# A windowed attention and a two-layer MLP on one core: other loads, exponentials and output order for the first batch

## The chip, the core and the metric

The kernel runs on one core of a Trainium2 chip. That core has TensorE (PE in the profile; PEld is its loading of weights), VectorE (DVE), ScalarE (ACT), GpSimd (POOL) and SyncE (SP). Here POOL issues nearly all transfers from HBM, because they change float32 to float16 on the way; SP issues the copies within SBUF of the first two batches and the output's stores. Sixteen DMA engines move the bytes of all queues. The metric is device time in microseconds (us), from launch to the last store.

## The reference

Eight batches, eight heads, 576 tokens, 64 numbers a head. Every query sees 32 keys: in heads 0 to 3 the 32 latest tokens, in heads 4 to 7 every fourth token back to 128. The rows of all heads then go through a two-layer MLP.

```python
rel = pos[:, None] - pos[None, :]
mask_plain = (rel >= 0) & (rel < window)
mask_dil = (rel >= 0) & (rel < window * dilation) & (rel % dilation == 0)
scores = np.where(masks[None], scale * q @ k.transpose(0, 1, 3, 2), -1e9)
attn = np.exp(scores - scores.max(-1, keepdims=True))
attn = attn / (attn.sum(-1, keepdims=True) + 1e-9)
x = (attn @ v).transpose(0, 2, 1, 3).reshape(B * S, H * D)   # 4608 x 512
h = x @ w_in                                                 # 512 x 2048
out = (h / (1 + np.exp(-h))) @ w_out                         # 2048 x 512
```

## The kernel before, in words

The order of instructions is written out by hand: each engine executes in the order of the Python calls. The plain heads are called z = 0, the dilated ones z = 1; for z = 1 the tokens are sorted into four classes, so that a class's window is contiguous. For each batch and z there are these steps: PE turns q and k (transposes against an identity), DVE and ACT copy them to `qT`, `kT` (z = 0) or `qC`, `kC` (z = 1); PE makes the scores; DVE scales, masks and finds the maximum (`ms`, `nm`); ACT takes the exponentials (`exps`, L459); DVE divides (`normal`, L472 to L475); PE turns the result (`turn`, L484), DVE copies it (`turned`, L492); PE multiplies with v (`values`); DVE copies into `xT` (`finish`).

`exps` has two forms. Where `shift` has subtracted the maximum on DVE (L441), one ACTIVATE covers all keys (L453) and the sums are a DVE reduction (L468). Otherwise ACT does one ACTIVATE with an accumulator for each block of 64 keys (L459), 8 to 12 for a part.

The MLP of a batch is `layer1` (16 groups of 128 hidden units, PE into a `big` PSUM tile, Silu on ACT into `gT`) and `layer2` (tiles of 128 tokens, 16 matmuls of 512 columns each, DVE copy, store by SP). `big` has 2 buffers of two banks, `ps` 4 of one bank. While the MLP of one batch runs, `plan_of(b)` puts the attention steps of later batches between its matmuls: `at(s, fn, ...)` runs `fn` at step s, where steps 0 to 15 are layer 1's groups and each step from 16 on is four matmuls of layer 2.

Batch 0 has nothing to hide behind, and is cut in two parts: tokens 0 to 255 and 256 to 575. Its layer 1 runs by part (`layer1_part`, L625; part 0 has steps -16 to -1, part 1 steps 0 to 15), and starts when the values of part 0 are in `xT`. Ahead of it stand, in this order on POOL's queue: q and k of part 0 (heads 4 to 7, then 0 to 3, `load_qk0`, L119), those of part 1, v of batch 0 (`load_v`: two dilated blocks L127, two short ones L134, the plain heads L138), four quarters of w_in (L175), q and k of batch 1 (L102), four quarters of w_out (L181), v of batch 1. A transfer of part 0 fills 32 partitions, one of part 1 fills 40. v arrives in the upper partitions of `vw`; `shift_v` copies it to the lower ones (L148, L153, L156, L158), for batch 0 on SP's queue in two groups, FIRST (what part 0 needs) and REST. `keep_busy` (L796) issues matmuls of the identity whose result nobody reads.

Of the kernel before, what the change touches and what calls it, by code (L numbers as in the profile page):

```python
# [8 lines left out]
F16 = mybir.dt.float16  # L9
F32 = mybir.dt.float32  # L10
# [4 lines left out]
P = 128  # L15
W = 32
DIL = 4
# [5 lines left out]
UR = 8  # L23
# [4 lines left out]
def kernel(  # L28
# [62 lines left out]
    def load_qk(b):  # L91

        for which in (0, 1):
            t = nat.tile([P, H * UR, D], F16, tag=f"n{which}", name=f"n{which}_{b}")
            u0, u1 = 2 * URS[0], 2 * (URS[0] + URS[1])
            qk[b, 0, which] = t[:, 0:u0].rearrange("p (h u) d -> p h u d", h=2)
            qk[b, 1, which] = t[:, u0:u1].rearrange("p (h u) d -> p h u d", h=2)
        for z in (1, 0):
            for which, src in ((1, k), (0, q)):
                for i in (0, 1):  # L100
                    h = 2 * (2 * z + i)
                    nc.gpsimd.dma_start(  # L102
                        out=qk[b, z, which][i * HF : i * HF + UPS[z]].rearrange("p h u d -> p h (u d)"),
                        in_=src[b, h : h + 2].rearrange("h (p u) d -> p h (u d)", u=URS[z]),
                    )

    def load_qk0(part, halves):

        t0, n = ((0, PA), (SA, PB))[part]
        if part not in qk0:  # L110
            qk0[part] = [
                nat.tile([P, H * UR, D], F16, tag=f"n{i}", name=f"n{i}_0{part}").rearrange(
                    "p (h u) d -> p h u d", h=H
                )
                for i in (0, 1)
            ]
        for h0, h1 in halves:
            for dst, src in ((qk0[part][1], k), (qk0[part][0], q)):
                nc.gpsimd.dma_start(  # L119
                    out=dst[0:n, h0:h1],  # L120
                    in_=src[0, h0:h1, t0 : t0 + n * UR].rearrange("h (p u) d -> p h (u d)", u=UR),
                )

    def load_v(b):
        vw = vws[b % 2]
        for m in (0, 1):
            nc.gpsimd.dma_start(  # L127
                out=vw[KB:P, NP + m * ND : NP + (m + 1) * ND].rearrange("p (h r) d -> p h (r d)", r=DIL),
                in_=v[b, HH:H, m * DIL * KB : (m + 1) * DIL * KB].rearrange("h (p r) d -> p h (r d)", r=DIL),
            )  # L130
        lo = CL - W - TL
        for n in (0, 1):
            c = NP + 2 * ND + 2 * n * DIL
            nc.gpsimd.dma_start(  # L134
                out=vw[n * KB : n * KB + W + TL, c : c + 2 * DIL].rearrange("p (h r) d -> p h (r d)", r=DIL),
                in_=v[b, HH + 2 * n : HH + 2 * n + 2, lo * DIL : S].rearrange("h (p r) d -> p h (r d)", r=DIL),
            )
        nc.gpsimd.dma_start(  # L138
            out=vw[KB:P, 0:NP].rearrange("r (h m) d -> r h m d", h=HH),
            in_=v[b, 0:HH].rearrange("h (m r) d -> r h m d", r=KB),  # L140
        )

    def shift_v(b, queue, parts):

# [49 lines left out]
    band = cpool.tile([P, KB], F32, name="band")  # L194
    nc.vector.memset(band[0:W], 0.0)
    clear_v(0, nc.vector)
    load_qk0(0, ((HH, H),))
    make_identity(nc, ident)

    nc.gpsimd.affine_select(  # L200
# [4 lines left out]
        out=band[0:W], in_=band[0:W], compare_op=ALU.is_ge, fill=NEG,  # L205
        base=W, pattern=[[-1, KB]], channel_multiplier=1,
    )
    load_qk0(0, ((0, HH),))
    load_qk0(1, ((HH, H), (0, HH)))
    load_v(0)  # L210
    shift_v(0, nc.sync, (FIRST, REST))
    for c in range(4):
        load_w_in(c)

    for kt, kc, qc in zip(kTs, kCs, qCs):
# [269 lines left out]
                t[:, i, :], a["pn", z, hi][:, 2 * i : 2 * i + 2].rearrange("p t c -> p (t c)"), ident  # L485
            )

    def turned(b, z, hi):
        a = att(b)
        n = width(b, z, hi) // 2  # L490
        pt = a["pt", z, hi] = ptp.tile([P, WM // 2, P], F16, tag="pt", name=f"ptT_{b}_{z}_{hi}")
        nc.vector.tensor_copy(pt[:, 0:n], a["ptT", z, hi][:, 0:n])  # L492

    def values(b, z):

# [52 lines left out]
            a["xs", z] = [ps.tile([P, 2, QB], F32, tag="ps", name=f"xs_0_{z}_0")]  # L548
            last_values(0, z, (0,))

    def finish0(z, part, copy=nc.vector.tensor_copy):
        a = att(0)
        run = QB * (DIL if z else 1)
        for e in (0, 1):
            f = lambda y: y.rearrange("d n (m e c) -> d n m e c", e=2, c=run)[:, :, :, e, :]
            copy(f(a["xT"][:, 2 * z : 2 * z + 2, part * SA : part * SA + SA]), f(a["x", z][e]))
        if part:
            last_finish(0, z, 0, copy)

    def last_values(b, z, es):  # L560

# [56 lines left out]
    def layer1_part(f, part):  # L618
# [12 lines left out]
                )  # L631
        nc.scalar.activation(gT[:, f : f + 2, c0:c1], h[:, :, 0 : c1 - c0], AF.Silu)  # L632

    def layer2(b, plan):

        tiles = range(0, 4) if b % 2 == 0 else range(4, 9)
        for x, t in enumerate(tiles):
            o = big.tile([P, 2, 512], F32, tag="big", name=f"o_{b}_{t}")[:, 0]
            for f in range(NFF):
                if f % 4 == 0:  # L640
                    plan(NFF + 4 * x + f // 4)
                nc.tensor.matmul(  # L642
                    o,
                    gT[:, f, t * P : (t + 1) * P],
                    w_out16[:, f, :],
                    start=(f == 0),
                    stop=(f == NFF - 1),
                )
            ob = o32.tile([P, DM], F32, tag="o32", name=f"ob_{b}_{t}")
            row = (b // 2) * 2 * S + t * P  # L650
            if (b, t) == (B - 1, 8):
                m = DM // 2
                ob2 = o32.tile([P, DM], F32, tag="o32", name="ob2")
                nc.vector.tensor_copy(ob[:, 0:m], o[:, 0:m])
                nc.sync.dma_start(out=out[row : row + P, 0:m], in_=ob[:, 0:m])
                nc.scalar.copy(ob2[:, 0:m], o[:, m:DM])
                nc.scalar.dma_start(out=out[row : row + P, m:DM], in_=ob2[:, 0:m])
            else:
                nc.vector.tensor_copy(ob, o)  # L659
                nc.sync.dma_start(out=out[row : row + P, :], in_=ob)  # L660

# [16 lines left out]
    def plan_of(b):  # L680
# [8 lines left out]

        if b == 0:  # L690

            at(-15, normal, 0, 1, 1)
            at(-14, turn, 0, 1, 1)
            at(-14, turned, 0, 1, 1)
            at(-13, normal, 0, 0, 1)
            at(-12, values0, 1, 1)
            at(-12, finish0, 1, 1)
            at(-10, turn, 0, 0, 1)
            at(-10, turned, 0, 0, 1)
            at(-8, last_values, 0, 1, (1,))  # L700
            at(-8, last_finish, 0, 1, 1)
            at(-7, values0, 0, 1)
            at(-7, finish0, 0, 1)
            at(-3, last_values, 0, 0, (1,))
            at(-3, last_finish, 0, 0, 1)
            transposes(at, 1, 1, -2)
            at(6, scores, 1, 1)
            for hi in (0, 1):
                at(6, shift, 1, 1, hi)
            transposes(at, 1, 0, 10)  # L710
            at(10, load_qk, 3)
            at(10, load_v, 2)
            at(10, shift_v, 2, nc.gpsimd, (ALL,))
            at(14, scores, 1, 0)
            at(14, shift_v, 1, nc.sync, (ALL,))
            all_exps(1, 1)
            all_exps(1, 0)
            later(at, 1, 1, (18, 20, 25, 27))
            later(at, 1, 0, (22, 25, 28, 30))
        elif b == 1:  # L720
            at(16, load_v, 3)
            at(16, shift_v, 3, nc.gpsimd, (ALL,))
            transposes(at, 2, 0, 2)
            transposes(at, 2, 1, 9)
            transposes(at, 3, 0, 15)
            at(6, scores, 2, 0)
            at(17, load_qk, 4)
            at(12, scores, 2, 1)
            all_exps(2, 0)
            all_exps(2, 1)  # L730
            at(17, scores, 3, 0)
# [31 lines left out]
        return plan  # L763


    turns = (nc.vector.tensor_copy, nc.scalar.copy)
    for n in range(4):
        transpose0(0, 2 + n // 2, 1 - n % 2, turns[n % 2])
    scores0(1, 0)
    for n in range(4):  # L770
        transpose0(0, n // 2, 1 - n % 2, turns[n % 2])
    exps(0, 1, 0)
    scores0(0, 0)
    load_qk(1)
    for c in range(4):
        load_w_out(c)
    clear_v(1, nc.gpsimd)
    load_v(1)
    exps(0, 0, 0)
    normal(0, 1, 0)  # L780
    for n in range(4):
        transpose0(1, 2 + n // 2, 1 - n % 2, turns[0])
    scores0(1, 1)
    turn(0, 1, 0)
    turned(0, 1, 0)
    exps(0, 1, 1)
    for n in range(4):
        transpose0(1, n // 2, 1 - n % 2, turns[0])
    load_qk(2)
    scores0(0, 1)  # L790
    busy = big.tile([P, 2, 512], F32, tag="big", name="busy")

    def keep_busy(n):

        for _ in range(n):
            nc.tensor.matmul(busy[:, 0, 0:P], ident, ident, start=True, stop=True)  # L796

    keep_busy(6)
    exps(0, 0, 1)
    normal(0, 0, 0)  # L800
    values0(1, 0)
    finish0(1, 0)
    keep_busy(9)
    turn(0, 0, 0)
    turned(0, 0, 0)
    keep_busy(3)
    values0(0, 0)
    finish0(0, 0)
    keep_busy(6)

    for b in range(B):
        plan = plan_of(b)
# [6 lines left out]
        else:  # L819
            for f in range(NFF):  # L820
                plan(f)
                layer1(b, f)
        layer2(b, plan)
        for s in range(NFF, 3 * NFF):
            plan(s)

# [29 lines left out]
```

## Time and profile before

| | us |
|---|---|
| median of 3 runs (329.48 to 333.6) | 330.9 |
| the profiled execution, its time | 333.1 |
| the profiled execution, its span | 331.3 |
| PE busy in the span | 311.7 (94%) |
| ACT, DVE, POOL busy | 217.5, 180.6, 88.3 |

The span runs from the first to the last instruction that is recorded; 1.8 us of the execution's time lie outside it. All times below are us from the start of the span. A row of a timeline gives start, duration, engine, line and operation, the tile written and read, the shape, the count, and in brackets how long the engine had been idle and what ended that. SPq and ACTq stand for an engine's issuing of transfers. In a list of transfers the last column is the median from issue to landing.

### The profile page before, as it was taken

The numbers are of one execution on the slowest core, as the hardware profiler recorded it, in microseconds if no ns is written. First come the engines' busy times: TensorE is split into PE (matmuls) and PEld (weight loads), VectorE is DVE, ScalarE is ACT, GpSimd is POOL, SyncE is SP. The second block draws the span as 40 slices with busy tenths as digits, with TensorE's granted clock in tenths as the row PEclk, the third lists the DMA queues.
The fourth block names the chain that finished last, engine by engine and source line by source line (L and its number), as shares of the span: only waits on it lengthen the run. The fifth ranks groups of instructions, "written<-read, shape, count | busy, mean of one in ns | idle before, by whom it ended". The sixth has DMA issues, their size and how long they took to land.

```text
span 331.3 us, 12022 instructions
## 1 busy us (share of the span) xinstructions
PE 311.7 (94%) x5240; PEld 203.6 (61%) x5240; DVE 180.6 (54%) x382; ACT 217.5 (66%) x747; POOL 88.3 (27%) x148
## 2 busy tenths in 40 slices
PE   4568999999799999999999999999999999999995
PEld 3446764577545677468745677468745676467642
DVE  7775378845568744774557444774557442530011
ACT  2693658446599947995699447995699447826300
POOL 8644836466100560046004430051000000000000
PEclk9999999999999999999999999999999999999999
DMA  6999999999701984189503990176001100110021
GB/s 83 156 213 212 193 192 230 216 185 131 110 35 63 136 141 78 63 101 168 82 35 87 183 142 4 63 98 110 2 34 66 65 4 0 63 65 2 0 95 67
DMA packets 45205, 32.90 MB, mean 99 GB/s; under 512 B 21888, under 2 KB 39808, under 8 KB 45152
## 3 DMA queue, kind: packets, MB, share of 16 engines
q0 software_dynamic: 38816, 21.74, 48.1%
q1 hardware_dynamic: 6192, 10.26, 8.7%
q8 instruction: 41, 0.67, 0.8%
q10 hardware_dynamic: 144, 0.13, 0.1%
q14 instruction: 12, 0.10, 0.1%
HBM read 37.75 MB, written 9.44 MB: 142 GB/s over the span
## 4 chain that ended last, share of the span: by engine, by line
PE 81%; DMA 6%; DVE 6%; ACT 3%; issue 2%; POOL 1%; SPq 0%; POOLq 0%; ACTq 0%
PE h L606 34%; PE o L642 32%; PE h L625 4%; PE t L260 3%; DMA vw<-in_v_dram 3%; PE x L517 2%; PE pt L484 2%; DMA vw<-vw 2%; ACT pe L459 2%; DMA n<-in_k_dram 2%; PE s L306 1%; PE s L318 1%; DVE pn L475 1%; DVE nm L431 1%; POOL n L119 1%
## 5 line engine op out<-in xcount | busy, mean ns | idle before, releaser
L642 PE MATMUL o<-w_out,gT 128*128 128x512 f16 x576 | 130.2, 380 | 0.0
L614 ACT ACTIVATE gT<-h 128x576 f16<-128x576 f32 x112 | 72.8, 650 | 69.3 <-PE h L606 68.6
L606 PE MATMUL h<-xT,w_in 128*128 128x288 f16 x896 | 115.4, 287 | 0.0
L606 PEld LDWEIGHTS <-w_in 128*128 128x128 f16 x896 | 85.7, 98 | 23.0
L459 ACT ACTIVATE pe<-ms,nm 128x64 f32<-128x64 f32 x284 | 94.2, 333 | 2.8 <-DVE nm L389 2.7
L642 PEld LDWEIGHTS <-gT 128*128 128x128 f16 x576 | 54.5, 98 | 60.8
L459 ACT ACTIVATION_READ_ACCUMULATOR pe<-ms,nm 128x1 f32 x284 | 53.0, 187 | 0.0
L659 DVE COPY ob<-o 128x512 f32<-128x512 f32 x35 | 24.1, 689 | 51.0 <-PE o L642 51.0
L415 DVE SCALAR_TENSOR_TENSOR ms<-s,mask 128x512 f32<-128x512 f32 x28 | 19.2, 687 | 39.0 <-PE ss L306 20.1
L127 POOL DMA_DIRECT2D vw<-in_v_dram x16 | 10.0, 632 | 90.1 <-PE x L517 89.9
L475 DVE TENSOR_TENSOR pn<-pe,r 128x640 f16<-128x640 f32 (+2 forms) x32 | 25.3, 792 | 1.1
L593 DVE CAST xT<-x 128x512 f16<-128x512 f32 x28 | 18.0, 686 | 12.5 <-PE xs L580 12.5
L431 DVE TENSOR_REDUCE nm<-ms 128x10 f32<-128x640 f32 (+1 forms) x28 | 22.0, 787 | 1.0
L492 DVE COPY ptT<-pt 128x640 f16<-128x640 f16 (+2 forms) x32 | 13.9, 469 | 9.9 <-PE pt L484 9.7
L102 POOL DMA_DIRECT2D n<-in_q_dram x28 | 16.4, 601 | 10.5 <-DMA w_in<-in_moe_w_in_dram 5.4
L632 ACT ACTIVATE gT<-h 128x512 f16<-128x512 f32 (+1 forms) x16 | 10.4, 650 | 13.3 <-PE h L625 13.3
L102 POOL DMA_DIRECT2D n<-in_k_dram x28 | 16.4, 597 | 8.6 <-DMA w_in<-in_moe_w_in_dram 3.6
L625 PE MATMUL h<-xT,w_in 128*128 128x256 f16 (+1 forms) x128 | 18.2, 295 | 0.1
L625 PEld LDWEIGHTS <-w_in 128*128 128x128 f16 x128 | 12.2, 101 | 3.6 <-issue 0.3
L260 PEld LDWEIGHTS <-n 64*64 64x64 f16 (+1 forms) x840 | 9.9, 101 | 6.4 <-issue 6.2
L260 PE MATMUL t<-ident,n 64*64 64x64 f16 (+1 forms) x840 | 11.6, 189 | 2.0 <-issue 2.0
L484 PE MATMUL pt<-ident,pn 128*128 128x128 f16 x152 | 12.4, 226 | 0.5 <-DVE pn L475 0.3
(82 smaller groups left out, 245.1 us busy)
## 6 DMA issues: line engine op xcount, KB each, us to landing
out_dram<-ob SPq DMA_DIRECT2D x35, 256.0 KB, 2.0
n<-in_k_dram POOLq DMA_DIRECT2D x28, 144.0 KB, 5.5
n<-in_q_dram POOLq DMA_DIRECT2D x28, 144.0 KB, 5.9
vw<-in_v_dram POOLq DMA_DIRECT2D x8, 288.0 KB, 6.1
vw<-in_v_dram POOLq DMA_DIRECT2D x16, 128.0 KB, 4.2
w_in<-in_moe_w_in_dram POOLq DMA_DIRECT2D x4, 512.0 KB, 10.0
w_out<-in_moe_w_out_dram POOLq DMA_DIRECT2D x4, 512.0 KB, 9.3
vw<-vw POOLq DMA_DIRECT2D x12, 128.0 KB, 3.5
```

The costliest lines, as they stand in the source:

```text
L102: nc.gpsimd.dma_start(out=qk[b, z, which][i * HF : i * HF + UPS[z]].rearrange("p h u d -> p h (u d)"), in_=src[b, h : h + 2].rearrange("h ...
L260: nc.tensor.transpose(dst, w, ident[r, r])
L415: nc.vector.scalar_tensor_tensor(out=ms[:, 0:8].rearrange("p (n t) c -> p n (t c)", n=2), in0=s[hi].rearrange("p n t c -> p n (t c)"), sca ...
L431: nc.vector.tensor_reduce(out=nm[:, 0:w], in_=ms[:, 0:w], axis=AX.X, op=ALU.max, negate=True)
L459: nc.scalar.activation(pe[:, t, :], ms[:, t, :], AF.Exp, bias=nm[:, t : t + 1], accum_out=l[:, t : t + 1],)
L475: nc.vector.tensor_tensor(pn[:, 0:w], a["pe", z, hi][:, 0:w], r[:, 0:w, None].broadcast_to([P, w, KB]), ALU.mult)
L484: nc.tensor.transpose(t[:, i, :], a["pn", z, hi][:, 2 * i : 2 * i + 2].rearrange("p t c -> p (t c)"), ident)
L606: nc.tensor.matmul(h[:, half, 0:HS], w_in16[:, c, f * P : f * P + P], xT[:, c, half * HS : half * HS + HS], start=(c == 0), stop=(c == MC ...
L614: nc.scalar.activation(gT[:, f, s0 : s0 + S].rearrange("p (a c) -> p a c", a=2), h[:, :, 0:HS], AF.Silu)
L625: nc.tensor.matmul(h[:, i, 0 : c1 - c0], w_in16[:, c, (f + i) * P : (f + i + 1) * P], xT[:, c, c0:c1], start=(c == 0), stop=(c == MC - 1),)
L642: nc.tensor.matmul(o, gT[:, f, t * P : (t + 1) * P], w_out16[:, f, :], start=(f == 0), stop=(f == NFF - 1),)
L659: nc.vector.tensor_copy(ob, o)
```

## The change

Loads of batch 0: `load_qk0` becomes one transfer for all eight heads, so four of them (k and q of part 0, k and q of part 1) in place of eight. `load_v` can be called for pieces; the new order on POOL's queue is q and k of both parts, v's first dilated block and its plain heads, w_in's first quarter, v's second block and the short ones, w_in's other quarters. Behind them: q and k of batch 1, the clearing of `vw`, two quarters of w_out, v of batch 1, the other two quarters of w_out, q and k of batch 2. From batch 2 on `load_qk` brings z = 0 first.

```diff
-    load_qk0(0, ((HH, H),))
+    load_qk0(0)
     make_identity(nc, ident)
...
-    load_qk0(0, ((0, HH),))
-    load_qk0(1, ((HH, H), (0, HH)))
-    load_v(0)
+    load_qk0(1)
+    load_v(0, ("first", "plain"))
+    load_w_in(0)
+    load_v(0, ("second", "short"))
     shift_v(0, nc.sync, (FIRST, REST))
-    for c in range(4):
+    for c in range(1, 4):
         load_w_in(c)
```

The stretch ahead of layer 1 is written anew. Part 1's scores are shifted on DVE, and its exponentials are two ACTIVATEs in place of 22. Copies are shared out otherwise (`turned` of part 0 and the q copies of part 1 on ACT; one half of `finish0` on each engine). Ahead of the first transposes stand 96 matmuls of the identity with 32 columns.

```diff
+    load_qk(1)
+    clear_v(1, nc.gpsimd)
+    load_w_out(0)
+    load_w_out(1)
+    load_v(1)
+    load_w_out(2)
+    load_w_out(3)
+    keep_busy(96, W)
+    transposes0(0, 1, (act, dve))
     scores0(1, 0)
+    transposes0(0, 0, (act, dve))
     exps(0, 1, 0)
     scores0(0, 0)
...
+    transposes0(1, 1, (act, dve))
     exps(0, 0, 0)
     normal(0, 1, 0)
...
     scores0(1, 1)
     turn(0, 1, 0)
-    turned(0, 1, 0)
+    turned(0, 1, 0, act)
+    transposes0(1, 0, (act, act))
+    normal(0, 0, 0)
+    turn(0, 0, 0)
+    turned(0, 0, 0, act)
+    shift(0, 1, 1)
     exps(0, 1, 1)
...
     scores0(0, 1)
+    shift(0, 0, 1)
+    keep_busy(12)
+    values0(1, 0)
+    finish0(1, 0, (dve, act))
+    values0(0, 0)
+    finish0(0, 0, (dve, act))
+    exps(0, 0, 1)
+    keep_busy(6)
+    load_qk(2)
```

Here `transposes0(part, z, copies)` turns k of both head pairs, then q of both, and gives `copies[0]` to q and `copies[1]` to k. `keep_busy(n, c)` takes a `big` tile of its own and issues n matmuls of c columns.

In the plan of batch 0 the steps of part 1 and of batch 1 are placed otherwise: `transposes(1, 1)` at 2 in place of -2, `scores(1, 1)` at 8 in place of 6, `transposes(1, 0)` at 13 in place of 10, `scores(1, 0)` at 17 in place of 14 and its exponentials at 17; `load_qk(3)`, `load_v(2)` and batch 2's shift at 15 in place of 10; batch 1's `turn` and `values` for z = 1 at 24 and 26 in place of 25 and 27. In the plan of batch 1 `transposes(2, 0)`, `scores(2, 0)`, `transposes(2, 1)` and `scores(2, 1)` stand at 4, 7, 10, 13 in place of 2, 6, 9, 12.

Layer 2 of batch 0 goes through the quarters of w_out in the outer loop and the four token tiles in the inner one, so that four sums stand open in both `big` buffers. The last token tile of the last batch is computed in two halves of 256 columns, each copied by DVE and stored by SP; before, one sum was copied half by DVE and half by ACT, and stored by both.

```diff
+    def layer2_first(plan):
+        o2 = [big.tile([P, 2, DM], F32, tag="big", name=f"o_0_{i}") for i in (0, 1)]
+        for c in range(4):
+            for t in range(4):
+                plan(NFF + 4 * c + t)
+                o = o2[t // 2][:, t % 2]
+                for f in range(4 * c, 4 * c + 4):
+                    nc.tensor.matmul(
+                        o, gT[:, f, t * P : (t + 1) * P], w_out16[:, f, :],
+                        start=(f == 0), stop=(f == NFF - 1),
+                    )
+                if c == 3:
+                    store(o, t * P, f"ob_0_{t}")
...
+            for part in (0, 1) if last else (None,):
+                for f in range(NFF):
...
+                    nc.tensor.matmul(
+                        o[:, part, 0:m] if last else o[:, 0],
+                        gT[:, f, t * P : (t + 1) * P],
+                        w_out16[:, f, part * m : (part + 1) * m] if last else w_out16[:, f, :],
+                        start=(f == 0), stop=(f == NFF - 1),
+                    )
+                if last:
+                    ob = o32.tile([P, m], F32, tag="o32", name=f"ob_last_{part}")
+                    nc.vector.tensor_copy(ob, o[:, part, 0:m])
+                    nc.sync.dma_start(out=out[row : row + P, part * m : (part + 1) * m], in_=ob)
```

## The prediction

> **What bounds the kernel now.** First the chain of waits over the first 60 us, since the change is there:
>
> ```profile
> 4.64 5.25 DMA n<-in_k_dram
> ...
> 10.17 8.33 DMA vw<-in_v_dram
> ...
> 19.23 7.14 DMA vw<-vw
> ...
> 26.41 0.56 PE x L543 x17
> 26.98 0.75 DVE xT L556 x2
> 27.73 0.04 issue
> 27.77 1.86 PE h L625 x8
> ```
>
> Columns: start, duration, what. Three transfers stand end to end: q,k of part 1 (their landing lets POOL issue v's plain heads: that is POOL's thirteenth transfer, and it waited for the fifth), v itself, and the copy within SBUF that `shift_v` makes. No exponential is in the chain; ACT ended its 22 blocks at 24.4, two us earlier. Then the window from the first layer-1 matmul to the end, and PE's waits in it:
>
> ```profile
> 27.77:331.30 303.53, 296.62 (x4800) 191.46 (x4799) 161.58 (x329) 200.61 (x665) 71.78 (x117) 1.00 0.53 94
> ```
>
> ```profile
> PE t L260 <- issue: 2.0, 1, 2.0
> PE s L306 <- DVE qT L264: 0.7, 1, 0.7
> PE pt L484 <- DVE pn L475: 0.3, 1, 0.3
> PE pt L484 <- DVE xT L593: 0.2, 1, 0.2
> ```
>
> PE is busy 296.6 of 303.5 us, and its waits sum to 3.2; the rest is the tail. So from 27.77 on the time is PE's work, which the change leaves as it is. Two things can move: when layer 1 starts, and those few gaps. The transfers, by size:
>
> ```profile
> w_in<-in_moe_w_in_dram POOLq DMA_DIRECT2D x4, 512.0 KB, 10.0
> n<-in_k_dram POOLq DMA_DIRECT2D x2, 160.0 KB, 6.8
> n<-in_q_dram POOLq DMA_DIRECT2D x2, 160.0 KB, 7.4
> n<-in_k_dram POOLq DMA_DIRECT2D x2, 128.0 KB, 2.9
> n<-in_q_dram POOLq DMA_DIRECT2D x2, 128.0 KB, 2.9
> ```
>
> The 40-partition pieces (160 KB) take over twice as long as the 32-partition ones (128 KB). And the pace and the tail, from the timeline:
>
> ```profile
> 27.77 1.86 PE L625 MATMUL h<-xT,w_in 128*128 128x256 f16 x8
> 29.93 1.04 PE L625 MATMUL h<-xT,w_in 128*128 128x256 f16 x8
> 327.78 0.42 DVE L654 COPY ob<-o 128x256 f32<-128x256 f32 x1 [2.76 <-PE o L642]
> 328.24 0.37 ACT L656 COPY ob<-o 128x256 f32<-128x256 f32 x1 [17.07 <-DVE ob L654]
> 328.64 0.38 ACTq L657 DMA_DIRECT2D out_dram<-ob  x1
> ```
>
> The same eight matmuls take 1.86 us at the start and 1.04 two us later: PE starts layer 1 at about half its later pace.
>
> **Loads, v first.** In front of the plain heads' landing (18.50) stand now 1,152 KB of q,k, 256 + 96 KB of other v blocks and the 288 KB themselves. The change moves 224 KB of the v blocks behind: at the 135 GB/s that the list of transfers gives as the mean of the first 20 us, 1.7 us. Part 0 comes as two transfers issued back to back (rows: 0.6 to 0.7 us each, from 1.33); now POOL makes identity and mask between the second and third (issues at 1.99 and 3.56), and the rate falls to 33 and 88 GB/s in two of that window's 0.5 us slices, from 182 before: another 0.8 us. The plain heads are then the sixth transfer, and wait for none. So v lands at about 18.5 - 2.5 = 16.0. The copy behind it is unchanged, with w_in still in the queues beside it: now 7.9 us from v's landing to its own (18.50 to 26.37); so it lands at 23.9. Bounds: no gain (26.4, first rival) to 22 (fourth part).
>
> **The copies of 40 partitions.** They speak against this. A 160 KB piece took 6.8 us where 128 KB took 2.9, and the change makes two pieces of 320 KB of them. The Trainium skill (DMA: Bandwidth & Descriptors, "Why a DMA increments its semaphore by 16 and not by 1") says that a transfer uses the largest number of engines up to 16 that divides its outermost dimensions: 40 partitions get ten engines, 32 get sixteen, and the next one starts where the last ended. The slow rows agree; by that rule two large pieces load four engines twice and v, which needs all, waits for those: the first rival. I take the 135 GB/s for all, since the mean holds the four slow pieces already.
>
> **Compute up to layer 1.** q of part 1 is whole at 15.4 now (the last of the four lets POOL go on to w_in's third quarter by then); 0.8 earlier is 14.6, and one large piece has its heads 4 to 7 no sooner than the rest, which now arrive at 12.1. I take 13.8. From there: 16 transposes 0.5; two q copies on ACT 2 x 0.48; part 0's second 8 exponentials 2.65, because ACT has them behind these copies; ACT's `turned` 0.45 and four copies at 0.48, 2.4 in all; scores 0.7; DVE `ms` 0.69 + 0.28, `nm` 0.82, and the added `shift` 0.78 (two 640-wide ones took 1.55): 2.6; a copy to `xT` 0.4. That ends at 24.0. What was 22 x 0.34 = 7.4 us of ACT is 0.81 + 0.68; the price is on DVE, two shifts and two sums, 0.93 + 0.78 + 0.95 + 0.82 = 3.5 us, of which only the 0.78 is ahead of layer 1. ACT's gain is thus spent: it was not the last to come, and its new copies stand behind q.
>
> Both chains end at 24; then v's last products 0.5, copies 0.4 (one each on DVE and ACT; 0.75 in a row before), waits 0.1 to 0.4. Layer 1 starts at 25.4 in place of 27.77: **-2.4**.
>
> **96 matmuls of the identity.** They run from about 3.2 (identity ready) until q lands, at 6.2. The nearest row is L288's transposes: 24 with the same 32 columns in 0.82 us, 0.034 each; 96 are 3.3 us, hidden by q. The other end, 0.127 each (nine of 128 columns took 1.14), is a rival. As for the pace: the Trainium skill (TensorE: Matmul & The Clock Gate, "Part 1") says that about 3.4 us of sustained matmuls double the clock and as long an idle lets it fall. The trace shows the doubling only at 29.8, after dense work, so I count 0; if it is up at layer 1's start, -0.8. The page's clock row says 9 throughout and does not show this.
>
> **Behind the start.** Silu's table load (1.28) and the last exponential (0.68) now follow the xT copies on ACT, where ACT was idle 3.9: Silu begins near 28.0, the third group of layer 1 needs its buffer at 27.5 to 29: **+0.3**. The wait of L306 for `qT` (0.7) goes, since scores(1,0) moves from step 14 to 17; but `ms` and `nm` of that step (3.2 us) then stand before batch 1's sums and divisions on DVE, which end some 9.1 us into layer 2 where step 24 comes at 8.4: 0.8 lost, and the two waits of 0.3 and 0.2 at that place are in it: -0.7 + 0.8 - 0.5 = **-0.4**. With four sums open, layer 1 of batch 1 gets its second buffer when the fourth copy is done, DVE being behind with two xT copies: **+0.3**. w_out's last quarter comes after v of batch 1, 5 us later than now (issued from 30.7, 9.3 to land, so about 48 in place of 43), and is needed 11 us into layer 2, near 59: nothing. The 2.0 of `issue` at L260 has no named cause and stands amid a dense row of short instructions; the change adds some 230 PE instructions and makes steps 10 to 17 denser. Between -2 (gone) and +2 (once more), I take 0, as it came once in 303 us.
>
> **Tail.** Now DVE 0.42, then ACT 0.37, then ACT's issue, one after another; after, the last half needs one copy: **-0.4**. 32 matmuls of 256 columns cost what 16 of 512 do (1.04 for 8 against 7.93 for 36, so 3.9 to 4.2 against 3.5, less the end of a row counted in the 1.04): 0 to +0.5, I take 0.
>
> Sum: -2.4 + 0.3 - 0.4 + 0.3 - 0.4 = -2.6. On the profiled execution's own 333.1 that is 330.5; it lies 2.2 above the median 330.9, so the forecast for the median is **328.3**.
>
> **Rivals.** (1) The transfers give nothing: two 40-partition pieces on the same few engines land q and v as late as now. Layer 1 at 27.7, sum -0.3: 330.6. For it the 6.8 and 7.4; against it that these pieces, issued one behind another, overlapped. 20%. (2) Slower: the warm-up holds PE. At 0.107 to 0.127 each, 96 matmuls end at 13.5 to 15.4 instead of 6.5; the first transposes wait, all steps of ACT and DVE shift by 7 to 9, of which 1 is slack, and layer 1 starts near 32 to 33.5: 335 to 336.5. It decides from 0.046 each (3.0 us to q and 1.4 of slack, over 96). Against it the 0.034 of L288; for it that the identity fills 128 rows where L288 filled 32. 8%. (3) Faster: v at 14.5, q at 11.5, so layer 1 at 22.6 (-5.2), pace doubled (-0.8), the 2.0 gone: with the rest, 322.7. 9%. (4) Small effects cancel otherwise, between 326 and 332: in the forecast.
>
> **Numbers.** Forecast 60%, rivals 20, 8 and 9, the rest spread. The measurement tells about 2% from no change, 6.6 us: under 324.3 is faster (rival 3 and a little: 0.09), over 337.5 slower (half of rival 2's upper end and what I do not see, 0.05), between them 0.86. Range 324.0 to 333.0: forecast with its unknowns (-0.8 and -2 for pace and gap, +2 for a second gap) and rival 1.
>
> **What would show it.** The chain of waits after: v's plain heads to about 16, copy to 24, L625's first row at 25.4, ACT's L453 rows of 0.8 and 0.7, 96 rows of `busy` ending by 6.5. L625 at 27.5 or later means rival 1; `busy` until 13, rival 2; PE waits over 6 us in all after the start, that I misjudged the plan.

## The result, and the profile after

The changed kernel takes 334.7 us (median of 13 runs, 333.2 to 335.0), the kernel before beside it 331.2 (13 runs, 329.5 to 334.4): ratio 1.0094, interval 1.0067 to 1.0121. Forecast were 328.3, with 333.0 as the range's upper end. It is a loss of 3 us where a gain of 2.6 was expected; it is about 1%, and the interval leaves out 1. In two kernels below the profiled execution is one far slower than the rest (`p96_before`, 458.2 us, with a clock of 0.65 from 30.8 us on, and `nbl_nopairs`, 335.8), and their ratios stand without it.

The profiled execution of the changed kernel has a span of 331.3, as that of before. First its chain of waits up to layer 1 (start, duration, what):

```profile
2.02 5.02 DMA n<-in_q_dram
...
8.62 1.81 PE t L295 x63
10.44 1.99 issue
12.43 0.19 PE t L295
...
17.50 0.44 PE t L295 x8
17.94 0.96 issue
...
22.92 0.41 PE x L542 x14
23.33 1.76 issue
25.09 0.78 PE x L542 x34
25.87 0.76 PE busy L795 x6
26.63 3.40 PE h L624 x21
```

The loads of part 1 and of v are gone from the chain. In their place stand three gaps of `issue`, 4.7 us, in which PE stood still in the middle of a row of equal instructions and waited for nothing that the profile names. Then PE's waits from layer 1 on, in the same kernel (line waited for, total, times, longest):

```profile
PE o L641 <- DVE ob L650: 2.0, 2, 1.2
PE pt L483 <- DVE pn L474: 1.1, 2, 0.8
PE s L305 <- issue: 0.8, 1, 0.8
PE o L665 <- DVE ob_last L674: 0.5, 1, 0.5
```

L641 is the new layer 2 of batch 0. Each sum is copied as soon as it ends, and the next sum's matmuls, which write the other half of the same PSUM tile, wait for that copy. L665 waits in the same way: the second half of the last tile for the copy of the first.

These are not whole stories yet: this execution (333.2) is the fastest of its 13, and the one shown of before (333.1) lies 1.9 over the median. So each kernel was profiled once more.

> The changed kernel as it is, a second profiled execution. The first one, 333.2, was the fastest of 13; their median is 334.7, and its profile cannot show the 1.5 us between. T2: a gap without a releaser of 1 to 2.5 us stands in the MLP of batch 0 or 1, or in batch 4's, that the first profile lacks, or is longer than the 0.8 there, at a count of 449 plus a multiple of 256. Otherwise (the start): layer 1 starts 1 to 2 us later than 26.5. Otherwise (T1): the waits for the copies are longer than 2.0 + 0.5.

> The kernel before as it is, a second profiled execution. The first took 333.1, 1.9 over the median of all its runs, with layer 1 at 27.8 and a gap of 2.0 behind it. If these two are the excess, an execution near 331.2 has layer 1 at 25.6 to 26.6 (as three kernels with the same beginning had) or no gap over 1 us after it.

They took 334.4 and 330.0. The chain's first row of layer 1, in before:

```profile
25.33 1.86 PE h L625 x8
```

and in the changed kernel, with what stands ahead of it:

```profile
9.51 2.91 issue
...
17.93 1.23 issue
...
23.60 1.76 issue
25.36 0.78 PE x L542 x37
26.14 0.76 PE busy L795 x6
26.89 3.21 PE h L624 x15
```

The first matmuls of layer 1 stand at 25.3 and 26.7 in the timelines, so in these two executions the change starts it 1.4 us later, not 2.4 earlier. The spans differ by 4.4 (332.6 against 328.2), and the other 3.0 lie behind the start: PE's waits there are 4.3 in the changed kernel (again 2.0 at L641, 1.1 at L483 and 0.5 at L665, and gaps of 0.7) and 1.7 in before, none over 0.7. The excess of the first profile of before was its start at 27.8 (the copies of v for part 0 landed at 26.4, in the second at 23.9) and the 2.0 of `issue`: neither is in the second one. The two make 4.4 and the spans differ by 3.1 only. Part of the rest is pace: the first two groups of eight matmuls of layer 1 took 1.86 and 1.91 us in the second profile, 1.86 and 1.04 in the first, so not all of an earlier start is won.

### The profile page after: what moved, and what is told of

Same layout as the page of the kernel before. It is cut to its first block, busy times and chain, and to the rows that moved or that the text cites. A ratio compares the mean times of both kernels' runs of the same rounds, so it can differ in the third digit from the quotient of the medians.

```text
span 331.3 us, 12192 instructions
## 1 busy us (share of the span) xinstructions
PE 313.2 (95%) x5346; PEld 206.7 (62%) x5346; DVE 180.5 (54%) x377; ACT 214.9 (65%) x714; POOL 86.0 (26%) x144
## 4 chain that ended last, share of the span: by engine, by line
PE 88%; DVE 4%; ACT 4%; issue 2%; DMA 2%; POOL 0%; POOLq 0%
PE h L605 34%; PE o L665 31%; PE h L624 5%; PE t L259 3%; ACT pe L458 3%; PE pt L483 3%; PE x L516 2%; PE o L641 2%; PE s L317 2%; DMA n<-in_q_dram 2%; PE s L305 1%; PE t L295 1%; DVE pn L474 1%; PE busy L795 1%; PE xs L579 1%
## 5 line engine op out<-in xcount | busy, mean ns | idle before, releaser
L665 PE MATMUL o<-w_out,gT 128*128 128x512 f16 (+1 forms) x528 | 115.8, 373 | 0.5 <-DVE ob_last L674 0.5
L605 PE MATMUL h<-xT,w_in 128*128 128x288 f16 x896 | 115.4, 286 | 0.0
L605 PEld LDWEIGHTS <-w_in 128*128 128x128 f16 x896 | 85.7, 98 | 22.9
L458 ACT ACTIVATE pe<-ms,nm 128x64 f32<-128x64 f32 x262 | 87.0, 334 | 0.6 <-DVE nm L430 0.5
L665 PEld LDWEIGHTS <-gT 128*128 128x128 f16 x528 | 50.1, 98 | 53.6 <-issue 0.7
L458 ACT ACTIVATION_READ_ACCUMULATOR pe<-ms,nm 128x1 f32 x262 | 49.1, 187 | 0.0
L414 DVE SCALAR_TENSOR_TENSOR ms<-s,mask 128x512 f32<-128x512 f32 x28 | 19.2, 687 | 37.4 <-PE ss L305 19.3
L474 DVE TENSOR_TENSOR pn<-pe,r 128x640 f16<-128x640 f32 (+2 forms) x32 | 25.3, 792 | 1.1
L491 DVE COPY ptT<-pt 128x640 f16<-128x640 f16 (+2 forms) x30 | 13.1, 473 | 9.8 <-PE pt L483 9.7
L641 PE MATMUL o<-w_out,gT 128*128 128x512 f16 x64 | 15.1, 379 | 2.0 <-DVE ob L650 2.0
L483 PE MATMUL pt<-ident,pn 128*128 128x128 f16 x152 | 12.2, 224 | 1.1 <-DVE pn L474 1.1
L259 PEld LDWEIGHTS <-n 64*64 64x64 f16 (+1 forms) x840 | 10.0, 101 | 4.5 <-issue 3.9
```

The source lines that it names most:

```text
L259: nc.tensor.transpose(dst, w, ident[r, r])
L458: nc.scalar.activation(pe[:, t, :], ms[:, t, :], AF.Exp, bias=nm[:, t : t + 1], accum_out=l[:, t : t + 1],)
L474: nc.vector.tensor_tensor(pn[:, 0:w], a["pe", z, hi][:, 0:w], r[:, 0:w, None].broadcast_to([P, w, KB]), ALU.mult)
L483: nc.tensor.transpose(t[:, i, :], a["pn", z, hi][:, 2 * i : 2 * i + 2].rearrange("p t c -> p (t c)"), ident)
L605: nc.tensor.matmul(h[:, half, 0:HS], w_in16[:, c, f * P : f * P + P], xT[:, c, half * HS : half * HS + HS], start=(c == 0), stop=(c == MC ...
L641: nc.tensor.matmul(o, gT[:, f, t * P : (t + 1) * P], w_out16[:, f, :], start=(f == 0), stop=(f == NFF - 1),)
```

## The experiments

Each ratio is to the kernel before, measured beside it, with its 95% interval; differences by the ratios are taken of 331 us. T1 is the wait for a copy, T2 the supply of PE's instructions, T3 the pace of PE, D the DVE chain ahead of L483.

**Waits for the neighbour's copy.** `e3_before_l2` is the kernel before with the new `layer2_first` and nothing else of the change. `e1_pairs` is the changed kernel with both sums of a tile finished before either is copied, and with a PSUM tile for each half of the last tile:

```diff
-                if c == 3:
-                    store(o, t * P, f"ob_0_{t}")
+                if c == 3 and t % 2:
+                    for t1 in (t - 1, t):
+                        store(o2[t // 2][:, t1 % 2], t1 * P, f"ob_0_{t1}")
...
+                if last:
+                    o = big.tile([P, 2, 512], F32, tag="big", name=f"o_{b}_{t}_{part}")
```

> The kernel before with one part of the change alone: layer 2 of batch 0 by quarters of w_out with four open sums. T1: two waits for copies at that line, 1.5 to 2.0 us together, and a time 1.5 to 2.0 us over the kernel before (ratio 1.005). T2: no loss before layer 1, which starts at 27.7 as before, and a ratio of 1.000 to 1.002.

> The changed kernel, but in layer 2 of batch 0 the two sums of one PSUM tile are both finished before either is copied, and the last token tile's halves lie in two PSUM tiles. Theory T1 (PE waits for the copy of the neighbouring sum in the same tile: 0.78 + 1.23 us at L641, 0.52 at L665): these three waits vanish and the time falls by 2.0 to 2.5 us against the changed kernel, to about 332.2 (ratio to the kernel before 1.002 to 1.004). Theory T2 (what costs is PE's supply of instructions before layer 1): waits vanish too, but the time stays at 334 or above, since PE then waits elsewhere. Neither: no change of the waits.

`e3_before_l2`: 334.5, ratio 1.0099 [1.0063, 1.0135]. One part of the change alone gives as large a loss as all of it, and its wait is that of L641 above, in PE's waits of this kernel:

```profile
PE o L642 <- DVE ob L651: 2.0, 2, 1.2
```

`e1_pairs`: 335.7, 1.013 [1.0091, 1.017]. Both waits are gone, and nothing is won: a wait of 2.3 appears at L605, layer 1 of batch 1, for the fourth copy.

**The store behind the copy.** `nb_pairs` is `e1_pairs` without the 96 first matmuls; `nb_pairs_late` also has batch 1's z = 1 `turn` and `values` at 25 and 27, as before.

> The changed kernel without the 96 warm-up matmuls and with the two sums of a PSUM tile finished before either is copied, the last halves in two tiles. T1: the three waits (0.78, 1.23, 0.52) go and the time falls by 2.0 to 2.5 us against the run without warm-up (333.3), to about 331, no slower than the kernel before. T2: at least one of the waits only hid a fetch of instructions, which shows as a gap without a releaser at a count of 449 + 256 k after layer 2 of batch 0, and the time stays between 332 and 334.

> As the run before it, and batch 1's turn and values for the dilated heads at steps 25 and 27, as in the kernel before, in place of 24 and 26. Theory D (DVE's chain is longer since the scores of the plain heads moved into layer 2, and PE waits 0.8 to 0.9 us for the last division at L483): that wait goes and 0.5 to 0.9 us with it. T2: the wait goes, the time does not follow it closely.

335.2, 1.012 [1.0075, 1.0166] and 336.4, 1.0159 [1.0113, 1.0206], both more than any theory expected. With the steps at 25 and 27 the wait for `pn` (0.9 in `nb_pairs`) is gone, as D expected, but no time with it; and L605 now waits 3.5 and 3.9. DVE's waits in `nb_pairs` from 55 to 72 us show on what:

```profile
DVE ob L651 <- DMA out_dram<-ob: 3.2, 1, 3.2
DVE ob L651 <- PE o L641: 1.2, 1, 1.2
```

and its output tiles at that place, the time from a store's issue to its landing:

```profile
DMA to landing us min/median/max: 3.5/5.8/6.0
```

Four copies come close together, the staging pool `o32` has three buffers, and the stores take 5.8 us amid the loads of the next batches (2.0 is the median over the whole changed kernel). The fourth copy waits for the first store. In the changed kernel, with its three buffers, no wait stands at L605: the waits for the neighbour had spread the copies, which would explain it. Four buffers were tried on the kernel before with the paired layer 2 (`l2_pairs_o4`), on `e1_pairs` (`e1_o4`), on `nb_pairs_late` (`nbl_o4`), and on the kernel before alone (`b_o4`).

> The kernel before, with the new layer 2 of batch 0, but the two sums of one PSUM tile are both finished before either is copied, and the output's staging pool has 4 buffers instead of 3. The new layer 2 alone, as the change writes it, gave a ratio of 1.0099. T1 (the loss is the wait of a sum for the copy of its neighbour in the same PSUM tile, 0.78 + 1.23, and, once that is gone, of a fourth copy for a staging buffer whose store is still in the transfer queues): both are gone, no row of L642 or of layer 1 of batch 1 waits for an output copy over 0.3 us, ratio 0.997 to 1.003. T2 (the loss is the supply of PE's instructions, and the order of the quarters only moved where it runs dry): the number of PE instructions is that of the kernel before, the gaps without a releaser stay at one or two in batch 0's and 1's MLP, and the ratio stays at 1.006 to 1.013 although the copies no longer stop PE.

> The changed kernel with the sums finished by pairs, the two last halves in PSUM tiles of their own, and 4 staging buffers. T1: the 2.0 of L641 and the 0.5 of L665 are gone and layer 1 of batch 1 no longer waits for a copy (2.3 with 3 buffers): 3.0 to 4.0 us less than the same kernel with 3 buffers (335.7), so 331.5 to 332.7, ratio 0.999 to 1.005. T2: the gaps without a releaser before layer 1 (about 4.7 us in sum in the changed kernel) and one of 0.8 to 2.4 in layer 2 of batch 0 stay, so the gain of 2.4 at the start does not show, and the ratio stays above 1.005.

> The changed kernel without the 96 first matmuls, sums by pairs, separate PSUM tiles for the last halves, batch 1's z = 1 turn and values one step later (25 and 27 as in the kernel before), 4 staging buffers. With 3 buffers it had a wait of 3.9 us of layer 1 of batch 1 for the fourth copy, and 336.4. T1: that wait goes whole, 331.5 to 332.8, ratio 1.001 to 1.006; below 1.000 if the earlier start (24.6) counts in full. T2: a gap without a releaser takes its place (the supply falls behind in the same stretch), the ratio stays at 1.006 or more.

> The kernel before with 4 staging buffers for the output in place of 3, nothing else: the control for the 0.9924 of the repaired kernel. In the profile of before no copy waits for a staging buffer, so T1 and T2 both expect no change: ratio 0.998 to 1.002. If the buffer alone gives 0.995 or less, the repaired kernel's gain is not the change's.

`l2_pairs_o4` 331.9, 1.0037 [1.0008, 1.0067]: of the 1.0099 of the new layer 2 nearly two thirds are gone, which is less than T1 expected and far more than T2 did. `e1_o4` 332.0, 1.0026 [1.0003, 1.0049], 3.4 less by the ratios than with three buffers. **`nbl_o4`, the repaired kernel, 328.6, 0.9924 [0.9899, 0.9949]: it beats both kernels.** `b_o4` 331.0, 0.9987 [0.9954, 1.002]: the buffer does nothing that shows for the kernel before. PE's waits in `nbl_o4` from layer 1 on:

```profile
PE ss L305 <- issue: 1.5, 1, 1.5
PE o L641 <- ACT gT L631: 1.2, 1, 1.2
PE pt L483 <- DVE pn L474: 0.3, 1, 0.3
PE t L259 <- issue: 0.2, 1, 0.2
PE h L605 <- DVE ob L651: 0.2, 1, 0.2
```

The window of this answer begins at 20 us; the first row is a gap at 19.9, ahead of layer 1, which starts at 24.6. Nothing waits over 0.3 for a copy. The 1.2 put down to ACT at the first matmul of layer 2 falls on instruction 1,729, of which more below. With three buffers the same kernel was 7.8 us longer by the ratios: the wait of 3.9, a gap of 1.8 at L259 and 6.8 us at half clock from 68.2 on (3.4 lost), 9.1 in all, are gone, and the 1.2 is new.

To price the shared tile in this version, `nbl_nopairs` copies each sum as it ends again.

> The repaired kernel with each of the four open sums of batch 0 copied as soon as it is finished, as the change has it, the two sums of a pair still in one PSUM tile. T1: the waits of L641 for a copy are back, 0.8 and 1.2, so 2.0 us or somewhat more: 330.4 to 331.6, ratio 0.998 to 1.002. T2: these waits give PE's supply time to catch up, gaps elsewhere shrink by as much: ratio 0.990 to 0.995.

330.2, 0.9961 [0.9934, 0.9987]: 1.2 us more than `nbl_o4` by the ratios, between the two expectations, with the waits 0.8 and 1.2 back. (The profile that shows them has other gaps besides: 1.5, 1.3 and 2.1.)

**The 96 first matmuls and the supply of instructions.** The gaps without a releaser have a pattern: counted over all of PE's instructions in the trace (matmuls, weight loads and 13 to 16 of its sequencer), each such gap of 0.5 us or more, in all the profiles, stands right behind instruction 449 or a multiple of 256 later (449, 705, 961, 1,473, 1,729, 1,985, 2,497, 3,265, 3,521 and 7,105). The 2.0 of before, at 86.9, stands behind number 3,265. The changed kernel's page has, under the DMA queues (packets, MB, share):

```profile
q8 instruction: 41, 0.67, 0.8%
```

41 packets of 16 KB for 10,708 PE instructions: 256 of 64 bytes in each. In the transfer records of its second profile such packets start at 10.06, 16.37 and 22.94, and PE resumes at 12.42, 19.16 and 25.36, 2.4 to 2.8 us later. So PE's program comes in pieces of 256 as DMA transfers during the run, and PE stops at a piece's end when the next is not ready. The Trainium skill (Runtime: NRT & Kernel Launch, "Instruction fetch mechanics") says that the stream is refilled in blocks of 16 KiB, 256 instructions, while the current one runs, and that a crossing is mostly hidden. The trace agrees on the block; with the queues full the crossing is not hidden.

The same records tell when a piece comes: there is one packet for each end of a piece. At the 49 such gaps of the first 70 us, over all profiles, the packet starts 3.3 to 4.7 us after PE has entered the 256 instructions ahead of that end, takes 0.9 to 1.4, and PE resumes 1.3 to 1.6 after it. After 240 us, with far fewer loads, the packet starts 0.4 us after that entry in the median. And at none of the 765 ends of pieces in these profiles (`p96_before` left out) does PE go on sooner than 1.2 us after the packet. So 256 instructions that PE runs through in under about 6 us amid full queues end in a gap.

To test this as a cause, tiny matmuls of zeros were put ahead of the first transposes in the kernel before, while PE waits for q anyway: 32 (64 instructions) and 96 (192).

```diff
+    for i in range(32):
+        nc.tensor.matmul(pad[0:W, 0, 0:W], zero[:, 0:W], zero[:, W : 2 * W], start=True, stop=True)
```

> The same with 32 tiny matmuls, 64 instructions. T2: another set of gaps, at the same counts of instructions, and another time, between 1 us less and 4 us more than the kernel before. T1: no change beyond 0.5 us, and the same as with 96.

> The kernel before, with nothing of the change, but with 96 tiny matmuls of zeros (32 by 32) as PE's first work, 192 instructions that run while PE has nothing to do but wait for q and k. T2 (PE's instructions come in pieces of 256, a piece takes some 6 us while the transfers' queues are full, and PE stalls where 256 instructions are used up sooner): each piece now ends 192 instructions earlier in the program, the gaps move to other places, still at the 449th, 705th, 961st... instruction, and the time moves by 1 to 4 us though no work was added to the path. T1 (the loss lies in the waits for the neighbouring sum) and any theory of work: the time stays within 0.5 us of the kernel before.

`p32_before`: 338.3, 1.0221 [1.0184, 1.0258]; `p96_before`: 331.4, 1.0004 [0.9984, 1.0023]. So not the amount counts but where the pieces' ends fall. T2's 1 to 4 us for the 96 did not come. In the trace of `p96_before` PE enters the 256 instructions ahead of the first end at 4.2 us, before most of the loads; the packet follows 0.7 later, and none of the three ends up to 30 us is a gap. PE's waits in `p32_before` from layer 1 on:

```profile
PE t L260 <- issue: 2.3, 1, 2.3
PE s L318 <- issue: 1.8, 1, 1.8
```

They are instructions 1,729 and 7,105. Each is followed by a stretch of half clock, as the windows of this kernel show (window; length; busy time of PE, PEld, DVE, ACT, POOL with counts; then the granted clock, the DMA share and GB/s):

```profile
44.00:47.20 3.20, 1.28 (x62) 0.86 (x61) 3.17 (x6) 1.41 (x3) 1.71 (x3) 1.00 1.88 177
47.40:50.80 3.40, 3.22 (x25) 1.94 (x25) 1.04 (x2) 1.15 (x2) 2.55 (x5) 0.50 1.29 223
50.80:54.00 3.20, 3.20 (x89) 2.11 (x88) 1.60 (x3) 1.29 (x3) 1.92 (x4) 1.00 1.17 242
```

3.4 us at half clock lose 1.7. Two gaps and two such stretches make 2.3 + 1.7 + 1.8 + 1.7 = 7.5; measured were 7.3 (1.0221 of 331).

The same edit on the repaired kernel, and the 96 of the change put back into it:

> The repaired kernel with 32 matmuls of 32 columns of zeros (64 instructions) ahead of its first transposes, before q has landed, so that their own time is hidden; nobody reads the result. T1: no change, ratio 0.990 to 0.995. T2: every instruction stands 64 places later against the pieces of 256, the gaps without a releaser move to other lines and change in size: by the same 64 instructions the kernel before lost 7 us in three of its stretches; a difference of at least 1 us to the repaired kernel, either way, and if a gap is 2 us or more, a stretch of half clock behind it (3.4 us, 1.7 lost).

> The repaired kernel (328.6, ratio 0.9924: sums by pairs, separate PSUM tiles for the last halves, 4 staging buffers, batch 1's z = 1 turn and values at 25 and 27, no first matmuls) with the 96 first matmuls of the changed kernel put back. It stands between the repaired kernel and the one of 332.0, which has the 96 and the steps 24 and 26. T2 (the 192 added instructions bring PE's supply to its next piece while the transfers of batch 0 fill the queues): layer 1 starts at 25.6 to 26.6 instead of 24.5, gaps without a releaser before it sum to 3.5 to 5 in place of about 1.5, ratio 0.997 to 1.002. T3 (the 96 keep the pace up): layer 1 at full pace from its start, ratio 0.990 or less. D (the steps 24 and 26 made the 332.0): ratio as without the 96, 0.990 to 0.995.

`nbl_p32`: 336.4, 1.0102 [1.0047, 1.0157], 5.9 more by the ratios, in a profile (333.0, the fastest of its runs) with gaps of 2.4 and 1.8 at 1,729 and 7,105. `nbl_busy96`: 332.8, 1.0023 [0.9997, 1.005], 3.3 more than without the 96. PE's waits in it from 8 us to the start of layer 1:

```profile
PE t L295 <- issue: 3.4, 2, 2.4
PE x L542 <- issue: 1.8, 1, 1.8
```

Layer 1 starts at 26.7 in place of 24.6, and the first 24 matmuls take longer, not less, in the timeline of this kernel:

```profile
26.75 5.08 PE L624 MATMUL h<-xT,w_in 128*128 128x256 f16 x24
```

than in `nbl_o4`:

```profile
24.59 3.53 PE L624 MATMUL h<-xT,w_in 128*128 128x256 f16 x24
```

T3 falls: in neither does layer 1 begin at full pace, and the full clock comes later with the 96 (from 31.5 us on, against 26.2; 28.1 to 31.5 in five profiles with them, 25.8 to 27.3 in five without). The later start (2.2) and these slower matmuls (1.5) make 3.7 of the 4.1 between the two profiles' spans. D falls too: `e1_o4`, the same kernel with the steps at 24 and 26, has 1.0026, so the steps are worth 0.1. The wait for `pn` is gone from `nbl_busy96`, but a gap of 0.9 behind instruction 2,497 has come.

The 192 instructions bring PE to the end of its first pieces while the queues are full of q, k, v and w_in: in `nbl_busy96` it enters the 256 ahead of the first end at 5.8 us, and goes on behind the first three ends at 12.7, 19.2 and 25.4, each a gap and all ahead of layer 1. In `nbl_o4` it enters them at 9.3 and passes the ends at 15.5, 21.4 and 29.4, the third within layer 1 and no gap. Two earlier runs on the changed kernel itself had the 96 left out (`e4_nobusy`) and replaced by 24 of 128 columns (`e2_busy24`).

> The changed kernel without the 96 warm-up matmuls (192 PE instructions less). T2: the fetches of instructions fall later in the program, the gap of 1.99 at 10.4 is gone or covered, and layer 1 starts 1 to 2 us earlier than 26.4; time 332.5 to 333.5. T3 (the warm-up keeps PE's pace up and is needed): layer 1 starts as now or later and its first groups stay at half pace longer than to 28.7; time 334.5 or more. T1 says nothing of the start and leaves the time at 334.6.

> The changed kernel with 24 matmuls of 128 columns as warm-up in place of 96 of 32 columns: about the same 2.6 us of PE, but 48 PE instructions in place of 192. T2 (the gaps of 1.99, 0.96 and 1.76 us that end at 12.4, 18.9 and 25.1 are PE waiting for its instructions, whose fetches stand 2.4 us ahead of each end): the gaps move or shrink, layer 1 starts 1 to 2 us earlier than 26.4, and the time falls by about as much. T1: the start may move, the waits at L641 stay at 2.0 and the time at 333.5 to 334.7. A third possibility, that the gaps are a wait for data: they stay where they are.

`e4_nobusy`: 333.3, 1.0067 [1.0034, 1.0101], layer 1 at 24.8: two us earlier, but only 0.9 less than the changed kernel by the ratios. `e2_busy24`: 337.0, 1.0179 [1.0139, 1.0219], although layer 1 starts at 24.9 and at full clock (from 24.9 on): gaps of 2.4 at L259 and 2.0 at L317 (again 7,105) and the waits of T1 take more than that gives. An early start was bought and lost.

**The front alone.** `nb_oldl2` is the changed kernel without the 96 and with layer 2 and the last tile as before.

> The changed kernel with layer 2 of batch 0 and the last tile as they were in the kernel before, and without the 96 first matmuls: the new loads, the new stretch ahead of layer 1 and the new plan alone. T1: layer 1 starts at 24.6 to 25.4 and nothing takes it back later, 328.5 to 330.5, ratio 0.991 to 0.998. T2: layer 1 starts early, but PE's instructions run dry once or twice in layer 1 and 2 of batch 0 (1 to 2.5 us each, at instruction counts of 449 plus a multiple of 256), so 330.5 to 333, ratio 0.998 to 1.006.

336.9, 1.0178 [1.013, 1.0225], against both theories. Layer 1 starts at 24.3; but PE's waits in it from there on begin with

```profile
PE o L641 <- DMA w_out<-in_moe_w_out_dram: 4.8, 2, 3.3
PE t L259 <- issue: 1.5, 1, 1.5
```

The old layer 2 wants all of w_out for its first token tile, and the new order of loads puts the second half behind v of batch 1. The quarters of layer 2 and the order of loads belong together; 6.8 us of half clock behind the wait lose another 3.4.

## Why the prediction was wrong, step by step

**"Layer 1 starts at 25.4 in place of 27.77: -2.4".** This is the step that failed most. The transfers did what it says, or better: v's plain heads landed at 16.2 (16.0 forecast), the copies behind them at 21.8 and 22.8 (23.9), q of part 1 at 12.9 (13.8; in the profile of before it landed at 14.7, not at the 15.4 that was read there). Yet PE's instructions were not there: 4.7 us of gaps in the first profile, 5.9 in the second, and a start at 26.5 and 26.7. The working has no term for them. Without the 96 matmuls the same front starts layer 1 at 24.3 to 24.8 in six kernels, earlier than forecast. And 27.77 was itself no typical start: the old front started it at 25.3, 25.7, 26.1 and 26.6 in four other profiles.

**"It lies 2.2 above the median 330.9, so the forecast for the median is 328.3".** The late start and the 2.0 gap were this excess (4.4 of waits, 3.1 of span, the rest in part pace, as above). The sum took 2.4 from the late start and the 2.2 once more. A gain of some 0.9 against a start near 26.3 would have followed from the same working, and a forecast near 330.

**"96 are 3.3 us, hidden by q", and rival 2.** Their duration was right: 96 took 2.75 us and ended at 6.0. Rival 2 (107 to 127 ns each) is refuted. But the warm-up cost 3.3 us in `nbl_busy96`, through the instructions that it puts ahead of everything, not through its time. Taken out of the changed kernel alone it gives back 0.9 (`e4_nobusy`), and gaps of 1.1 and 0.5 behind instructions 1,729 and 3,265 have come.

**"The 2.0 of `issue` at L260 has no named cause ... I take 0".** It had one, and the page named its queue: `instruction`. -2 to +2 held for one gap; in the changed kernel they were three, ahead of layer 1, where the prediction did not look for them.

**"With four sums open, layer 1 of batch 1 gets its second buffer when the fourth copy is done ...: +0.3".** The place was right and the wait another: 2.0 us inside layer 2, since two sums share a PSUM tile and the wait is on the tile. Four open sums in two tiles were seen; whose copy blocks whom was not. The price of separate copies in the repaired kernel is 1.2. In the tail the same wait costs 0.5, where 0 was taken for the halves; the one copy at the end is 0.4 shorter, as forecast.

**"-0.7 + 0.8 - 0.5 = -0.4".** The wait for `qT` is gone and one of 0.8 for `pn` came; of the two of 0.3 and 0.2 one stays. About -0.1. **Table load +0.3**: no wait for it appears in the changed kernel. **w_out's last quarter, "nothing"**: right, because of the new order in layer 2 (`nb_oldl2`): it landed at 53.6 (48 forecast; before at 46.2, not 43) and was needed at 63.1.

**Rival 1** (the transfers give nothing) is refuted by the landings: the 320 KB pieces of 40 partitions took 7.8 and 8.5 us, little over the 6.8 and 7.4 of 160 KB, and v's plain heads landed at 16.2, against 18.5 and 17.1 in the two profiles of before. **Rival 3** (faster) had the right direction for the start, 24.6 in `nbl_o4`, but not its size (22.6).

Of the 5.6 us between the changed kernel and `nbl_o4`, by runs that follow one another: sums by pairs, the last halves apart and the fourth buffer together 2.25 (1.0094 to 1.0026, `e1_o4`), the steps 25 and 27 0.1 (to 1.0023, `nbl_busy96`), the 96 3.3 (to 0.9924). Another order gives other shares, as `e4_nobusy` shows, so these are no fixed prices. What makes a packet start 3.3 to 4.7 us late amid loads, and why the clock fell behind some gaps and not behind others, was not settled.

## What to carry to other kernels

A gap without a releaser inside a row of equal instructions is worth a count: if the counts differ by multiples of a fixed number, it is the program's supply, and each instruction put ahead of a stretch with full queues, however short and hidden, brings the ends of the pieces forward. Here a piece of 256 ran dry where PE was through with it in under about 6 us amid full queues; an end that falls into long matmuls, or ahead of the loads, cost nothing. When several sums share a PSUM tile, finish all of them before the first is copied, and count the staging buffers against the stores then in flight. Before a term is taken from one profile, ask whether that execution's distance from the median is the same term.

## What the runs showed of the hardware

- PE's instructions come in pieces of 256. At the gaps of the first 70 us a piece's transfer started 3.3 to 4.7 us after PE had entered the piece before, and PE went on 2.2 to 2.9 us after that start. 64 instructions more moved the time by 5.9 and 7.3 us in two kernels, 192 more by 3.3 in one and by nothing that shows in another.
- After a gap of about 2 us PE may run 3.4 us at half clock (twice in `p32_before`), but need not: `nbl_p32` had gaps of 2.4 and 1.8 and a clock of 1.00 from 25.1 us on. The Trainium skill (TensorE: Matmul & The Clock Gate, "Part 1") has windows of 3,413 ns that run freely of the kernel; the 3.41 agrees. In `p32_before` 2.1 and 1.8 us of the gaps lie in the window just ahead of the fall; a window's edge cuts the 2.4 of `nbl_p32` in two halves of 1.2. But the 1.8 of `nbl_p32` lies whole in one window, and the clock held, so where the limit lies stays open; the gaps ahead of the falls are shorter than the 3.4 us of idle that the prediction counts with. In the second profile of the changed kernel the clock was full from 6.3 to 9.8 us, behind the 96 matmuls, and fell as the gap of 2.9 began; in no other profile is such a stretch recorded.
- A store of 256 KB took 5.8 us at the end of batch 0, amid loads, against a median of 2.0 over the changed kernel.
